# Seven half-size products with three accumulating on one bank and fewer sums on DVE

## Chip, cores and metric

The kernel runs on one core of a Trainium2 chip. The metric is the device time of one execution in microseconds; the medians below are over three runs.

## What is computed

Causal attention with a decay (2 x 8 heads, 576 positions, width 64), then a mixture of 4 experts (1152 tokens, 512 wide, 1024 inner), then a gated layer (inner width 1536). Cut to the layers that the change touches:

```python
def _moe_ref(x, domain_probs, w1, w2):
    p = domain_probs / (domain_probs.sum(-1, keepdims=True) + 1e-09)
    out = np.zeros((N, D), dtype=np.float32)
    for e in range(E):
        h = np.maximum(x @ w1[e], 0.0)
        out += p[:, e:e + 1] * (h @ w2[e])
    return out
def _moe2_ref(x, w_gate, w_val, w_out):
    g = x @ w_gate
    silu = g * (1.0 / (1.0 + np.exp(-g)))
    return (silu * (x @ w_val) @ w_out).astype(np.float32)
```

## The kernel before

Every float32 operand is split into a high and a low part, and each product is three matmuls (high x high, high x low, low x high). The inner width is worked in pieces of 256, the tokens in two halves of 512 and 640. A *stage* is one piece of width and one half of the tokens: the inward products x @ w (its items), then the outward products (6 matmuls for each 128 tokens, in two items of 3). The first stages belong to the mixture, the last ones to the gated layer; below these are called the first and the second stage of the kernel.

An inward product [256 wide x 512 deep] x [512 deep x tokens] is done as a 2 x 2 block product in seven half-size products instead of eight (`seven`, L1070): the weights' and x's halves and their sums are made ahead, and the seven results are added up to the four blocks c11, c12, c21, c22 of the result, which lie side by side in one SBUF tile "cc". The intermediate sums are called u1, u2, u3, u4. Each of the seven products is 6 matmuls of 256 or 320 columns (half of the tokens' half) into a PSUM bank of its own ("h", five banks in rotation). Product 0 is copied out to u1 by ACT or DVE; the other results are added on DVE straight from their banks: c11 = u1 + 1, u2 = u1 + 2, u4 = u2 + 3, u3 = u2 + 4, c12 = u4 + 5, c22 = u4 + 4, c21 = u3 + 6 (`total`, L1108, and the lambda at L1132): seven DVE sums and a copy for each set. `rest` then works on each half of "cc": relu and split in the first stage (`moe1_seven`, L1204), sigmoid, multiply and split in the second (`moe2_in`, L1341), where a stage has two sets, gate and value.

The order of the work is written out while the kernel is built: a greedy planner (`Plan`) holds a clock for each engine with cost estimates, takes the task that can start first (rank settles ties), and lets a copy marked "av" go to the engine that bids less, ACT or DVE (`held`, 1 us in this part, is added to DVE's bid). After an operation a dependent one on another engine, or on the same engine other than PE, is taken to be ready LINK later (0.13 us for ACT and DVE, 0.2 for PE). A `Ring` is the planner's count of free buffers: `take` needs a free one, `give` hands one back. PE's own order is fixed: each item hangs on the last (`dense_pe`, L960).

In `stages` (L1427) the inward items of a stage are merged with the outward items of the stage before: `merge` (L99) spreads the inward items evenly from 0 to 1 and the outward ones from 0.75 to 1 (LAG). So in a first-stage set five products come first, then an outward item, product number five, more outward items, product six, and the rest. In a second-stage stage the seven gate products come without outward items between them, and the value products from the fourth on with them. Stages of a piece that was begun before all tokens were there have fewer outward items to merge. The first piece of the second stage and the last stage have orders of their own (L1453 to L1464).

Of the kernel before, what the change touches and what calls it, by code (L numbers as in the profile page):

```python
# [8 lines left out]
F32 = mybir.dt.float32  # L9
# [8 lines left out]
P = 128  # L18
# [3 lines left out]
HALF = 512  # L22
# [258 lines left out]
def attention_moe_swiglu(ctx, tc, q_early, q_late, k, v, s, dp, w1, w2, wg, wv, wo, out):  # L281
# [691 lines left out]
    def needs_x(t0, t1):  # L973
        if t0 in x_ready:
            return x_ready[t0]
        return [x for g in range(len(groups)) if place[g] < t1 for x in done_x[g]]
# [88 lines left out]
        late["sums"] = [x for y in done.values() for x in y]  # L1065


    SEVEN = [((0, 0), (0, 0)), ((0, 1), (1, 0)), (0, 1), (2, 0), (1, 2), (3, (1, 1)), ((1, 1), 3)]

    def seven(w, st, rest):  # L1070


        t0, n = st.t0, (st.t1 - st.t0) // 2
        box, done, banks = {}, {}, {}
        x_ = late["T", t0]

        def item(i):
            A, X = SEVEN[i]

            def run():  # L1080
                hp = banks[i] = bank("h")[:, :n]
                for c in range(2):
                    if isinstance(A, tuple):
                        wh, wl = (y[:, 2 * A[1] + c, A[0] * P:A[0] * P + P] for y in w.ops)
                    else:
                        wh, wl = (y[:, A, c, :] for y in w.sums)
                    if isinstance(X, tuple):
                        a = t0 + X[1] * n
                        h, l = (y[:, 2 * X[0] + c, a:a + n] for y in (xh, xl))
                    else:  # L1090
                        h, l = (x_[y][:, X, c, :] for y in "hl")
                    nc.tensor.matmul(hp, wh, h, start=c == 0, stop=False)  # L1092
                    nc.tensor.matmul(hp, wh, l, start=False, stop=False)  # L1093
                    nc.tensor.matmul(hp, wl, h, start=False, stop=c == 1)  # L1094

            def make(last):
                deps = [w.done[A[1]] if isinstance(A, tuple) else w.sums_done[A]]
                deps += needs_x(t0, t0 + 2 * n) if isinstance(X, tuple) else x_["done"][X]
                give = [(w.first, w.parts_ring), (w.first, ring("ws"))] if last and i == 6 else []
                done[i] = t = dense_pe(6 * pe(n), run, deps, take=[ring("h")], give=give)  # L1100
                finish(i, t)
                return t
            return make

        def part(k):
            return box["c"][:, k * n:k * n + n]

        def total(k, x, i, deps, spent=False):  # L1108

            def run():  # L1110
                nc.vector.tensor_tensor(part(k), part(x), banks[i], op=ALU.add)  # L1111
            return add("dve", 0.12 + 0.00113 * n, run, deps, give=[(done[i], ring("h"))] if spent else [], rank=prompt())


        def finish(i, t):
            if i == 0:
                def copy(on):
                    box["c"] = late["t"].tile([P, 2 * (N - HALF)], F32, name="cc", tag="cc", bufs=2)[:, :4 * n]
                    move(on, part(1), banks[0])
                done["u1"] = any_of("av", "bank", n, copy, [t], take=[ring("cc")], give=[(t, ring("h"))], rank=prompt())  # L1120
            elif i == 1:
                done["c11"] = total(0, 1, 1, [t, done["u1"]], True)
            elif i == 2:
                done["u2"] = total(1, 1, 2, [t, done["c11"]], True)
            elif i == 3:
                done["u4"] = total(3, 1, 3, [t, done["u2"]], True)
            elif i == 4:
                done["u3"] = total(2, 1, 4, [t, done["u2"]])
            elif i == 5:
                done["c12"] = total(1, 3, 5, [t, done["u4"], done["u3"]], True)  # L1130
                rest(0, [done["c11"], done["c12"]], done["u1"], lambda: box["c"], n)
                done["c22"] = add("dve", 0.12 + 0.00113 * n, lambda: nc.vector.tensor_tensor(part(3), part(3), banks[4], op=ALU.add),  # L1132
                                  [done["c12"]], give=[(done[4], ring("h"))], rank=prompt())
            elif i == 6:
                c21 = total(2, 2, 6, [t, done["u3"]], True)
                rest(1, [done["c22"], c21], done["u1"], lambda: box["c"], n)
        return [item(i) for i in range(7)]

    def order(st):

# [200 lines left out]
    def moe2_in(wgt, wvt, st):  # L1341
# [22 lines left out]
        def val(f, deps, owner, src, n):  # L1364
# [11 lines left out]
            lows.append(st.lows[f, st.t0, 2 * n])  # L1376
            if len(lows) == 2:
                add(None, 0.0, None, lows, give=[(box["ts"], ring("sg")), (owner, ring("cc"))])
        return seven(wgt, st, gate) + seven(wvt, st, val)

    def moe2_out(w, st, first, last):
        items = []
# [44 lines left out]
    def stages():  # L1427
# [3 lines left out]
        for i, t0, t1, lastone in jobs():  # L1431
# [21 lines left out]
            if i == 1000 and t0 == 0:  # L1453

                items = items[:3] + prev + items[3:]
            elif i == 1000:

                items = [items[x] for x in (0, 1, 7, 8)] + merge(items[2:7] + items[9:], prev)
            elif i == 1000 + len(wide) - 1 and t0:
                items = items + prev  # L1460
            elif prev:
                items = merge(items, prev)
# [125 lines left out]
```

## Time and profile before

| | us |
|---|---|
| runs | 717.32, 718.48, 718.18; median 718.18 |
| the profiled execution | 719.07 |
| its span from the first to the last instruction | 717.2 |
| PE busy | 698.9 (97%) |
| DVE busy | 557.2 (78%) |
| ACT busy | 358.2 (50%) |
| POOL busy | 463.2 (65%) |

Attention takes the span's first part; the first set of seven products starts at 198.7 us, the second stage at about 492 us. In the rows, "h" is a bank for inward products and "o" one for outward products; "cc" is the tile of the four blocks; "hh" and "hl" are mostly the high and low part of the inner activations; "wah", "wsh" and the like are parts of weights and of their sums; "acc_a" and "acc_b" are the output's accumulators. L1092 to L1094 are the matmuls of a set, L1154 to L1156 those of an outward item, L1111 and L1132 the DVE sums, L327 a copy on ACT. A matmul's busy time runs to its modelled end, and the next one starts before that, so the pace of PE is read from starts.

### The profile page before, as it was taken

The numbers are of one execution on the slowest core, as the hardware profiler recorded it, in microseconds if no ns is written. First come the engines' busy times: TensorE is split into PE (matmuls) and PEld (weight loads), VectorE is DVE, ScalarE is ACT, GpSimd is POOL, SyncE is SP. The second block draws the span as 40 slices with busy tenths as digits, with TensorE's granted clock in tenths as the row PEclk, the third lists the DMA queues.
The fourth block names the chain that finished last, engine by engine and source line by source line (L and its number), as shares of the span: only waits on it lengthen the run. The fifth ranks groups of instructions, "written<-read, shape, count | busy, mean of one in ns | idle before, by whom it ended". The sixth has DMA issues, their size and how long they took to land.

```text
span 717.2 us, 11928 instructions
## 1 busy us (share of the span) xinstructions
PE 698.9 (97%) x4280; PEld 607.2 (85%) x4280; DVE 557.2 (78%) x1081; ACT 358.2 (50%) x757; POOL 463.2 (65%) x436
## 2 busy tenths in 40 slices
PE   8899999999999999999999999999999999999997
PEld 6676666787898989898989888997989999999996
DVE  5686575797278899999999999766884777787665
ACT  5787777423444545555565654655644424233210
POOL 3743242599366667666767678799899868585321
PEclk9999999999999999999999999999999999999999
DMA  8794642112204445465446553222121202010003
GB/s 206 241 306 125 205 135 85 31 58 71 106 0 148 147 157 168 147 207 166 147 160 194 188 186 103 65 86 89 39 80 31 82 23 74 30 31 1 1 1 133
DMA packets 31452, 79.80 MB, mean 111 GB/s; under 512 B 3568, under 2 KB 9216, under 8 KB 31392
## 3 DMA queue, kind: packets, MB, share of 16 engines
q1 hardware_dynamic: 31248, 78.90, 34.4%
q8 instruction: 34, 0.56, 0.3%
q14 instruction: 26, 0.21, 0.1%
q10 hardware_dynamic: 144, 0.13, 0.1%
HBM read 67.16 MB, written 11.85 MB: 110 GB/s over the span
## 4 chain that ended last, share of the span: by engine, by line
PE 74%; DVE 12%; POOL 5%; issue 4%; ACT 4%; DMA 0%; DVEq 0%; ACTq 0%; POOLq 0%
PE h L1092 10%; PE h L1094 10%; PE h L1093 10%; PE o L1154 10%; PE o L1155 10%; PE o L1156 10%; PE tp L598 2%; PE po L657 2%; PE sp L527 2%; DVE tt L1031 1%; ACT ns L553 1%; PE h L992 1%; DVE cc L1111 1%; PE h L994 1%; PE h L993 1%
## 5 line engine op out<-in xcount | busy, mean ns | idle before, releaser
L1111 DVE TENSOR_TENSOR cc<-cc,h 128x320 f32<-128x320 f32 (+1 forms) x282 | 124.9, 452 | 49.3 <-PE h L1094 43.0
L1154 PE MATMUL o<-woh,hh 128*128 128x512 f32 x396 | 157.3, 397 | 2.9 <-DVE acc_a L1242 1.6
L1156 PE MATMUL o<-woh,hl 128*128 128x512 f32 x396 | 154.7, 391 | 1.7 <-DVE hl L340 1.7
L1155 PE MATMUL o<-wol,hh 128*128 128x512 f32 x396 | 155.8, 393 | 0.0
L1092 PE MATMUL h<-xh,wsh 128*128 128x320 f32 (+1 forms) x312 | 92.9, 298 | 0.0
L1094 PE MATMUL h<-xh,wsl 128*128 128x320 f32 (+1 forms) x312 | 92.8, 297 | 0.0
L1093 PE MATMUL h<-xl,wsh 128*128 128x320 f32 (+1 forms) x312 | 92.7, 297 | 0.0
L340 POOL TENSOR_TENSOR wal<-raw,wah 128x512 fp32r<-128x512 f32 (+1 forms) x58 | 70.8, 1230 | 32.4 <-ACT wah L327 31.4
L1156 PEld LDWEIGHTS o<-woh,hl 128*128 128x128 f32 x396 | 74.4, 188 | 18.6 <-DVE hl L340 2.1
L340 POOL TENSOR_TENSOR wol<-raw,woh 128x512 fp32r<-128x512 f32 x54 | 79.2, 1475 | 15.0 <-ACT woh L327 14.5
L1154 PEld LDWEIGHTS o<-woh,hh 128*128 128x128 f32 x396 | 74.5, 188 | 16.6 <-DVE acc_a L1242 2.3
L1155 PEld LDWEIGHTS o<-wol,hh 128*128 128x128 f32 x396 | 74.5, 188 | 10.8
L1211 ACT ACTIVATE cc<-cc 128x640 f32<-128x640 f32 (+1 forms) x46 | 32.1, 698 | 91.7 <-DVE cc L1111 91.6
L340 POOL TENSOR_TENSOR hl<-cc,hh 128x512 fp32r<-128x512 f32 (+1 forms) x28 | 41.9, 1498 | 52.8 <-ACT hh L1214 52.6
L1092 PE MATMUL h<-xh,wah 128*128 128x320 f32 (+1 forms) x234 | 69.4, 297 | 0.0
L1094 PE MATMUL h<-xh,wal 128*128 128x320 f32 (+1 forms) x234 | 69.4, 296 | 0.0
L1093 PE MATMUL h<-xl,wah 128*128 128x320 f32 (+1 forms) x234 | 69.3, 296 | 0.0
L340 POOL TENSOR_TENSOR wsl<-sf,wsh 128x512 fp32r<-128x512 f32 x44 | 66.8, 1537 | 0.8 <-ACT wsh L327 0.8
L1242 DVE SCALAR_TENSOR_TENSOR acc_b<-o,pr,acc_b 128x512 f32<-128x512 f32 x75 | 55.5, 743 | 8.4 <-PE o L1156 8.1
L1092 PEld LDWEIGHTS h<-xh,wsh 128*128 128x128 f32 x312 | 58.9, 189 | 1.5
L1093 PEld LDWEIGHTS h<-xl,wsh 128*128 128x128 f32 x312 | 59.0, 189 | 1.4
L1094 PEld LDWEIGHTS h<-xh,wsl 128*128 128x128 f32 x312 | 59.0, 189 | 0.0
(146 smaller groups left out, 1667.8 us busy)
## 6 DMA issues: line engine op xcount, KB each, us to landing
raw<-in_w SPq DMA_DIRECT2D x42, 512.0 KB, 5.0
n<-hl SPq DMA_DIRECT2D x36, 256.0 KB, 2.3
raw<-n SPq DMA_DIRECT2D x18, 512.0 KB, 3.3
hh<-in_wg SPq DMA_DIRECT2D x12, 512.0 KB, 4.2
hh<-in_wv SPq DMA_DIRECT2D x12, 512.0 KB, 4.0
hh<-in_wo SPq DMA_DIRECT2D x12, 512.0 KB, 3.9
dql<-rows SPq DMA_DIRECT2D x8, 512.0 KB, 5.1
vr<-in_v SPq DMA_DIRECT2D x4, 640.0 KB, 4.4
```

What stands on the lines that cost most here:

```text
L340: {"v": nc.vector, "p": nc.gpsimd}[e].tensor_tensor(to, x, f32(y), op=ALU.subtract)
L527: nc.tensor.matmul(sp[j][:, at:at + w], Q[half[j], x], K[half[j], :w], start=True, stop=False)
L598: nc.tensor.transpose(tp[:kn, x * P:x * P + P], box["ns"][lane][:, at + c * P:at + c * P + kn], ident)
L1092: nc.tensor.matmul(hp, wh, h, start=c == 0, stop=False)
L1093: nc.tensor.matmul(hp, wh, l, start=False, stop=False)
L1094: nc.tensor.matmul(hp, wl, h, start=False, stop=c == 1)
L1111: nc.vector.tensor_tensor(part(k), part(x), banks[i], op=ALU.add)
L1154: nc.tensor.matmul(op, hh[:, f, ts], wh[:, f, :], start=f == 0, stop=False)
L1155: nc.tensor.matmul(op, hh[:, f, ts], wl[:, f, :], start=False, stop=False)
L1156: nc.tensor.matmul(op, hl[:, f, ts], wh[:, f, :], start=False, stop=f == NF - 1)
L1211: nc.scalar.activation(src()[:, o], src()[:, o], AF.Relu)
L1242: nc.vector.scalar_tensor_tensor(acc(t), bank_(), sc, acc(t), op0=ALU.mult, op1=ALU.add)
```

## The change

Products 0, 2 and 3 go onto one bank. Product 0 is copied out as u1; product 2 then accumulates onto the same bank, which so holds u2, and is copied out; product 3 accumulates onto that, which gives u4, and is copied out. The DVE sums u2 and u4 are no more, and two copies come, free for ACT or DVE. In the first stage (`join`) product 6 accumulates onto the bank of product 4 once c22 has read it, which makes the sum u3 unnecessary: four DVE sums. In the second stage u3 stays as a sum and product 6 has its own bank: five DVE sums. Each accumulating product waits for the read before it (`READ`). The order of the seven is 0, 1, 5, 2, 4, 3, 6 instead of 0 to 6. The first piece of the second stage gets another order for its second half. Cut to its core:

```diff
+    TURN = (0, 1, 5, 2, 4, 3, 6)
     SEVEN = [((0, 0), (0, 0)), ((0, 1), (1, 0)), (0, 1), (2, 0), (1, 2), (3, (1, 1)), ((1, 1), 3)]
 
-    def seven(w, st, rest):
+    def seven(w, st, rest, join=True):
...
+        ONTO = (None, None, 0, 0, None, None, 4 if join else None)
+        READ = ((), (), ("u1",), ("u2",), (), (), ("c22",) if join else ())
...
             def run():
-                hp = banks[i] = bank("h")[:, :n]
+                if ONTO[i] is None:
+                    banks[i] = bank("h")[:, :n]
+                hp = banks[i] = banks[i if ONTO[i] is None else ONTO[i]]
...
-                    nc.tensor.matmul(hp, wh, h, start=c == 0, stop=False)
-                    nc.tensor.matmul(hp, wh, l, start=False, stop=False)
-                    nc.tensor.matmul(hp, wl, h, start=False, stop=c == 1)
+                    for x, (a, b) in enumerate(((wh, h), (wh, l), (wl, h))):
+                        nc.tensor.matmul(hp, a, b, start=not x and not c and ONTO[i] is None, stop=x == 2 and c == 1, skip_group_check=i in (0, 2, 3) or join and i in (4, 6))
...
+                deps += [done[x] for x in READ[i]]
...
-                done[i] = t = dense_pe(6 * pe(n), run, deps, take=[ring("h")], give=give)
+                done[i] = t = dense_pe(6 * pe(n), run, deps, take=[ring("h")] if ONTO[i] is None else [], give=give)
...
+        def taken(k, i, deps, **kw):
+
+            def copy(on):
+                if "c" not in box:
+                    box["c"] = late["t"].tile([P, 2 * (N - HALF)], F32, name="cc", tag="cc", bufs=2)[:, :4 * n]
+                move(on, part(k), banks[i])
+            return any_of("av", "bank", n, copy, deps, rank=prompt(), **kw)
 
         def finish(i, t):
             if i == 0:
...
+                done["u1"] = taken(1, 0, [t], take=[ring("cc")])
             elif i == 1:
-                done["c11"] = total(0, 1, 1, [t, done["u1"]], True)
+                done["c11"] = total(0, 1, 1, [t, done["u1"]], 1)
             elif i == 2:
-                done["u2"] = total(1, 1, 2, [t, done["c11"]], True)
+                done["u2"] = taken(2, 2, [t])
             elif i == 3:
-                done["u4"] = total(3, 1, 3, [t, done["u2"]], True)
-            elif i == 4:
-                done["u3"] = total(2, 1, 4, [t, done["u2"]])
-            elif i == 5:
-                done["c12"] = total(1, 3, 5, [t, done["u4"], done["u3"]], True)
+                done["u4"] = taken(3, 3, [t], give=[(done[0], ring("h"))])
+                done["c12"] = total(1, 3, 5, [done["u4"], done["c11"], done[5]], 5)
                 rest(0, [done["c11"], done["c12"]], done["u1"], lambda: box["c"], n)
...
+                done["c22"] = total(3, 3, 4, [done["c12"], done[4]])
+                if not join:
+                    done["u3"] = total(2, 2, 4, [done["c22"]], 4)
             elif i == 6:
-                c21 = total(2, 2, 6, [t, done["u3"]], True)
-                rest(1, [done["c22"], c21], done["u1"], lambda: box["c"], n)
-        return [item(i) for i in range(7)]
+                done["c21"] = total(2, 2, 6, [t, done["c22" if join else "u3"]], 4 if join else 6)
+                rest(1, [done["c22"], done["c21"]], done["u1"], lambda: box["c"], n)
+        return [item(i) for i in TURN]
...
-        return seven(wgt, st, gate) + seven(wvt, st, val)
+        return seven(wgt, st, gate, False) + seven(wvt, st, val, False)
...
-                items = [items[x] for x in (0, 1, 7, 8)] + merge(items[2:7] + items[9:], prev)
+                items = items[:3] + merge(items[3:], prev)
```

## Rows read from the trace of the kernel before

**Rows 1.** The page's part 1: busy us, share of the span, instructions.
```profile
PE 698.9 (97%) x4280; PEld 607.2 (85%) x4280; DVE 557.2 (78%) x1081; ACT 358.2 (50%) x757; POOL 463.2 (65%) x436
```

**Rows 2.** PE's waits from 198 us on: line, releaser, us, times, longest.
```profile
PE o L1156 <- DVE hl L340: 1.7, 1, 1.7
PE o L1270 <- DVE xl L1281: 1.5, 1, 1.5
PE h L1092 <- DVE cc L1111: 1.0, 1, 1.0
PE o L1154 <- DVE acc_b L1242: 0.4, 1, 0.4
PE o L1154 <- DVE acc_a L1242: 0.3, 1, 0.3
PE h L1092 <- ACT cc L327: 0.2, 1, 0.2
```

**Rows 3.** Table of stretches: us, busy by engine (x), PEclk, DMA share, GB/s.
```profile
198.00:500.00 302.00, 299.33 (x1738) 268.74 (x1736) 268.76 (x417) 163.19 (x297) 218.93 (x182) 1.00 0.43 140
500.00:545.00 45.00, 42.41 (x285) 39.61 (x286) 35.62 (x67) 23.68 (x52) 43.04 (x44) 1.00 0.20 60
545.00:717.00 172.00, 168.53 (x1055) 156.26 (x1053) 120.40 (x210) 50.02 (x96) 100.60 (x87) 1.00 0.12 39
```

**Rows 4.** Groups by line and shape: count, busy us, mean ns, idle before.
```profile
L1111 DVE TENSOR_TENSOR cc<-cc,h 128x320 f32<-128x320 f32 x156 | 74.2, 483 | 31.3 <-PE h L1094 26.8 <-ACT cc L327 0.8 <-ACT woh L327 0.7
L1111 DVE TENSOR_TENSOR cc<-cc,h 128x256 f32<-128x256 f32 x126 | 50.7, 414 | 18.1 <-PE h L1094 16.2
```

**Rows 5.** Timeline, gate set at 320 columns: start, us, engine, line, tiles.
```profile
588.09 0.31 PE L1094 MATMUL h<-xh,wsl 128*128 128x320 f32 x1
588.44 0.49 DVE L1111 TENSOR_TENSOR cc<-cc,h 128x320 f32<-128x320 f32 x1 [0.39 <-PE h L1094]
588.97 0.31 PE L1094 MATMUL h<-xh,wsl 128*128 128x320 f32 x1
```

**Rows 6.** Timeline, gate set at 256 columns.
```profile
568.82 0.37 ACT L327 COPY cc<-h 128x256 f32<-128x256 f32 x1 [0.26 <-PE h L1094]
...
570.58 0.28 PE L1094 MATMUL h<-xh,wsl 128*128 128x256 f32 x1
...
571.30 0.28 PE L1094 MATMUL h<-xh,wsl 128*128 128x256 f32 x1
```

**Rows 7.** Timeline around a PE wait for a copy, ACT, PEld and PE.
```profile
519.37 0.42 ACT L327 COPY cc<-h 128x320 f32<-128x320 f32 x1
519.84 0.19 PEld L1092 LDWEIGHTS h<-xh,hl 128*128 128x128 f32 x1 [0.49 <-ACT cc L327]
519.84 0.42 PE L1092 MATMUL h<-xh,hl 128*128 128x320 f32 x1 [0.23 <-ACT cc L327]
```

**Rows 8.** Timeline, late set of the first stage, PE and DVE.
```profile
449.40 0.31 PE L1094 MATMUL h<-xh,wsl 128*128 128x320 f32 x1
450.70 0.40 PE L1156 MATMUL o<-woh,hl 128*128 128x512 f32 x1
450.94 0.30 PE L1092 MATMUL h<-xh,wah 128*128 128x320 f32 x1
...
450.27 0.49 DVE L1132 TENSOR_TENSOR cc<-cc,h 128x320 f32<-128x320 f32 x1
450.68 0.74 DVE L1242 SCALAR_TENSOR_TENSOR acc_a<-o,pr,acc_a 128x512 f32<-128x512 f32 x1
```

**Rows 9.** Timeline near the end, POOL and PE.
```profile
705.70 1.56 POOL L340 TENSOR_TENSOR hl<-sg,hh 128x640 fp32r<-128x640 f32 x1 [1.53 <-ACT hh L327]
707.70 0.39 PE L1156 MATMUL o<-woh,hl 128*128 128x512 f32 x1
```

**Rows 10.** Timeline, turn between the stages, PE and ACT.
```profile
532.45 0.28 PE L1094 MATMUL h<-xh,wal 128*128 128x256 f32 x1
...
534.11 0.39 ACT L327 COPY cc<-h 128x256 f32<-128x256 f32 x1
```

More of the change, by code (lines that the diff above doesn't have):

```diff
@@ L1106, in part, with total @@
             return box["c"][:, k * n:k * n + n]
-        def total(k, x, i, deps, spent=False):
+        def total(k, x, i, deps, spent=None):
             def run():
                 nc.vector.tensor_tensor(part(k), part(x), banks[i], op=ALU.add)
-            return add("dve", 0.12 + 0.00113 * n, run, deps, give=[(done[i], ring("h"))] if spent else [], rank=prompt())
+            return add("dve", 0.12 + 0.00113 * n, run, deps, give=[] if spent is None else [(done[spent], ring("h"))], rank=prompt())
@@ L1115, in finish @@
+        def taken(k, i, deps, **kw):
[4 more added lines that the diff above has]
+            return any_of("av", "bank", n, copy, deps, rank=prompt(), **kw)
         def finish(i, t):
             if i == 0:
-                def copy(on):
-                    box["c"] = late["t"].tile([P, 2 * (N - HALF)], F32, name="cc", tag="cc", bufs=2)[:, :4 * n]
-                    move(on, part(1), banks[0])
@@ L1120, in finish @@
-                done["u1"] = any_of("av", "bank", n, copy, [t], take=[ring("cc")], give=[(t, ring("h"))], rank=prompt())
+                done["u1"] = taken(1, 0, [t], take=[ring("cc")])
             elif i == 1:
-                done["c11"] = total(0, 1, 1, [t, done["u1"]], True)
+                done["c11"] = total(0, 1, 1, [t, done["u1"]], 1)
             elif i == 2:
-                done["u2"] = total(1, 1, 2, [t, done["c11"]], True)
+                done["u2"] = taken(2, 2, [t])
             elif i == 3:
-                done["u4"] = total(3, 1, 3, [t, done["u2"]], True)
-            elif i == 4:
-                done["u3"] = total(2, 1, 4, [t, done["u2"]])
-            elif i == 5:
-                done["c12"] = total(1, 3, 5, [t, done["u4"], done["u3"]], True)
+                done["u4"] = taken(3, 3, [t], give=[(done[0], ring("h"))])
@@ L1131, in finish @@
+                done["c12"] = total(1, 3, 5, [done["u4"], done["c11"], done[5]], 5)
                 rest(0, [done["c11"], done["c12"]], done["u1"], lambda: box["c"], n)
-                done["c22"] = add("dve", 0.12 + 0.00113 * n, lambda: nc.vector.tensor_tensor(part(3), part(3), banks[4], op=ALU.add),
-                                  [done["c12"]], give=[(done[4], ring("h"))], rank=prompt())
+                done["c22"] = total(3, 3, 4, [done["c12"], done[4]])
+                if not join:
+                    done["u3"] = total(2, 2, 4, [done["c22"]], 4)
```

## The prediction

> **What bounds the kernel now.** I read the busy line of the page first: PE is busy 97% of the span, DVE 78%, ACT 50% [rows 1]. Then the table of stretches, cut where the sets of seven products run: from 198 us on PE is busy 510.3 of 519 us at full granted clock, while DVE is at 89% (268.8 of 302) in the first stage, 79% in the turn from one stage to the other and 70% (120.4 of 172) in the last; ACT is at 54%, 53% and 29% [rows 3]. So PE is the bound, and its instruction count doesn't change: 47 sets of 42 matmuls stay. The only room is PE's waits, so the list of these came third: six single waits after 198 us, 1.7 + 1.5 + 1.0 + 0.4 + 0.3 + 0.2 = 5.1 us, five of them on DVE, one on ACT [rows 2]. A wait also lays the weight load open: the matmul after the wait at 519.84 takes 0.42 us, where one in a stream takes 0.31 [rows 5, 7]; with the matmul that follows about 0.2 us for each, 1.2 in all. So 6.3 us is the most that the change can win, 0.9%, unless it makes PE's stream itself shorter, which it doesn't.
>
> **What leaves and what comes.** The first stage has 23 sets, the second 24 (6 pieces of width, 2 halves of the tokens, gate and value). Of 7 DVE sums 4 are left in the first and 5 in the second: 3 x 23 + 2 x 24 = 117 sums go, 66 at 320 columns (0.483 us) and 51 at 256 (0.414) [rows 4]: 31.9 + 21.1 = 53 us off DVE, an eighth of its 425 us in this part. Two copies a set come, which the planner gives to ACT unless ACT is far behind (HELD2 adds 1 us to DVE's bid): 52 x 0.42 + 42 x 0.37 = 37 us on ACT [rows 6, 7], which has the room on average. All of this lies beside PE; what matters is which waits go and which come.
>
> **Waits that can go (gains).** Evictions of bank "o" that DVE does late, 0.4 + 0.3, with their weight loads 1.1 us: they come from DVE's backlog in the first stage, and a sum fewer in three should end most; I take 0.8 (0 to 1.1). The wait of 1.7 for "hl" has a chain through DVE, ACT and DVE again, behind integer work of the narrowing that stays; I take 0.8 (0 to 1.9). The 1.5 for "xl" hangs on the transposes of the turn, which no sum feeds; 0.3 (0 to 1.7). The two waits for a bank "h", 1.0 + 0.2, with their loads 1.6: a set takes 4 or 5 banks instead of 7, so these as such go: 1.6. Sum 3.5 us.
>
> **Waits that come (losses).** Each accumulating product now waits for a copy, and PE is in order: all that is behind it waits too, both products and output matmuls.
>
> *Product 3 behind the copy of u2.* Product 4 lies between. At 320 columns a product's last matmul starts at 588.09 and ends at 588.40; a reader reacts in 0.04 (the sum at 588.44) [rows 5]; the copy takes 0.42, and PE's weight load starts 0.05 after its end (519.79 to 519.84) [rows 7]: 588.91. The weight load of the product after the next goes with the matmul at 588.97 [rows 5]. So 0.06 us are left. At 256 columns: 570.58 + 0.28 + 0.04 + 0.37 + 0.05 = 571.32, wanted at 571.30 [rows 6]: 0.02 late, or some 0.05 with a slower reaction. This holds where nothing else is merged in between: the 12 gate sets, and two value sets (the first piece's first half and the last of all). In the first stage and in the other value sets at least one output item of 3 x 0.24 us (450.70 to 450.94 for one of its matmuls [rows 8]) lies between as well, so some 0.7 us is left. The same gap again: five banks are taken by a set of the second stage, so the value's product 0 takes the bank of the gate's product 0, free only after the copy of u4, with product 6 between: 12 more. 26 places in all, half at 256 columns: 13 x 0.05 = 0.7 us if ACT is idle; when ACT is in the middle of another operation, up to that one's length each (0.4 us and more). ACT at 29% there [rows 3] speaks for the low end: 0.7 (0 to 4).
>
> *Product 6 behind c22 (first stage only).* The chain is product 3, copy of u4, c12, c22. In 21 of the 23 sets five or more output items (15 x 0.24 = 3.6 us) lie between 3 and 6, enough: 0.04 + 0.42 + 0.05 + 0.48 + 0.74 + 0.48 + 0.05 = 2.3 us, with an eviction of 0.74 between the sums [rows 4, 7, 8]. An integer operation of the narrowing in front as well takes it to the edge in some: 0.4 us in all (0 to 3). In two sets, of stages that have only four output items to merge, two lie between. There (rows of 449.4 on, where the last matmul of the product in this place ends at 449.71): copy until 450.17, c12 until 450.71, eviction until 451.45, c22 until 451.9; product 6 wants its weight load at 450.70 [rows 8]. Wait 1.2 us; 0.4 if c22 goes ahead of the eviction. The planner takes the eviction first, as it adds 0.13 us (LINK) behind c12 and the eviction is ready by then. 2 x 1.2 = 2.4; but the first of the two stands just ahead of the "hl" wait of 1.7, in which part of it drowns: 1.8 (0.6 to 2.6).
>
> *Product 2 behind the copy of u1.* Two products lie between, so one more (0.72 or 0.88 us [rows 5, 6]) than above: 0.7 to 0.9 us beyond the copy. In the turn between the stages ACT is often later: at 534.11 the copy starts 1.38 us after product 0 ends (532.73) [rows 10]. With three such places, and u2 and u4 in the same queue behind casts: 1.5 us (0 to 3).
>
> *The end.* In the last stage value product 3 ends where 5 did, but c12 waits for a copy (0.5 us more) and u3 is one more sum (0.45) ahead of c21, whose multiply, cast and low part end in "hl" at 707.26; the matmul that reads it starts at 707.70, its load a matmul (0.24) earlier [rows 9]. 0.9 late against 0.2 of room: 0.7 at most, nothing if the planner gives the multiply to POOL, idle there: 0.4.
>
> *Orders that move.* Product 5 is third now and needs weight sum 3 two places earlier; weights are made up to four ahead (AHEAD) and before their stage begins, so nothing. In the second stage's first piece product 5 leads instead of 2 (own quarter of x instead of a sum: earlier ready), and in its second half three products lead instead of four; sums of x are ready before. Nothing, from -0.5 to 0.5. No DMA and no SP instruction moves.
>
> Losses: 0.7 + 0.4 + 1.8 + 1.5 + 0.4 = 4.8 us. Net 4.8 - 3.5 = +1.3. The profiled execution is 719.07 (span 717.2 and 1.9 around it), so 720.4 for it; the median is 0.9 lower, and the forecast for it 718.18 + 1.3 = 719.5.
>
> The Trainium skill, Perfetto Trace Analysis, Optimizing Tensor Performance, speaks against this change: independent matmul groups should rotate through different banks so that the reading of one overlaps the next. The rows agree so far that a product in a stream has 0.06 us left at best; what the rule would make of the time is rival (e). The same page, Optimizing Scalar/DVE Operations, says that work of a full DVE may well go to ScalarE, which is the case for it; DVE here is full only in part of the first stage.
>
> **Rivals.** (a) *Relief wins.* DVE's backlog sets all five DVE waits, the copies find ACT idle, and c22 goes ahead: gains 5.5 (all but part of "xl"), losses 0.4 + 0 + 0.8 + 0.7 + 0.4 = 2.3: -3.2, 715.0. For it: 89% on DVE in the first stage. Against: six waits in 519 us show that the planner already keeps the backlog off PE. (b) *The joined bank is the new bound.* In the dense part of the first stage, where DVE is fullest, c22 comes behind narrowing and evictions in most of the 21 sets; from a lag of about 3.4 us on it holds PE, and at 0.2 us in each this adds 4: 723.5. (c) *Nothing to speak of*: copies hidden, waits where they were: 718.2 +- 1. (d) *The clock falls.* With short waits in each set the granted clock could go to its lower level, 1.2 of 2.4 GHz; against it, it was 1.00 in all three stretches, the one with the waits of 1.7 and 1.5 us too [rows 3]. The 42.4 us of PE work in the middle stretch at half speed would be +42: 760. The Trainium skill, TensorE: Matmul & The Clock Gate, A second HAM failure mode, tells of a kernel whose cycling through banks made the clock swing; the trace here shows none of it. (e) *Bare copies.* Were nothing of a copy hidden, each of some 117 new waits (2 a set, 23 more at product 6) would cost 0.42 + 0.09: 60 us, 778. Against it, a product of 0.72 or 0.88 us lies between in all of them [rows 5, 6].
>
> **How the numbers follow.** Forecast (waits trade places, 718.0 to 721.5): 0.44, half of it under 719.6. (a) 0.30, (b) 0.16, (c) 0.09, (d) and (e) together 0.01. A measurement here tells 0.2% (1.4 us) from no change. Faster by more: (a) and a little of (c), 0.31. Within: half the forecast and most of (c), 0.30. Slower: the other half, (b), (d) and (e), 0.39. Range from (a) to (b): 714.8 to 723.5; the forecast alone 718.0 to 721.5.
>
> **What would show it.** DVE near 504 us and ACT near 395 on the page; 212 DVE sums and 141 copies; no wait of PE for "h" on DVE's sums but at product 6; two waits of about 1.2 us at product 6 in the stages around 430 and 450 us; waits of under 0.1 us on ACT's copies in the gate sets after 545 us. I am wrong if PE's waits after 198 us add up to under 3 us (a), or if product 6 waits in most sets of the first stage (b), or if the granted clock is under 1.

## The result, and the profile after

The changed kernel takes 725.45 us (median of four runs, 724.97 to 726.25) against 718.33 for the kernel before beside it: 1.0102 times as long, interval 1.0084 to 1.0119. The same kernel again, in a later comparison with more runs: 723.79 against 717.99, 1.0082 (1.0065 to 1.0099). So it is slower by some 6 to 7 us, where 719.5 was forecast, with 723.5 as the upper end.

The page of the changed kernel, part 1 (busy us, share of the span, instructions), answers to [rows 1]:

```profile
PE 706.4 (98%) x4280; PEld 609.2 (84%) x4280; DVE 531.4 (73%) x978; ACT 393.2 (54%) x851; POOL 449.6 (62%) x422
```

Groups by line and shape, after (L1116 the DVE sums, L327 the copies out of the banks of a set; x is their count, then busy us and mean ns), against [rows 4]:

```profile
L1116 DVE TENSOR_TENSOR cc<-cc,h 128x320 f32<-128x320 f32 x116 | 54.5, 481 | 48.7 <-ACT cc L327 42.9 <-PE h L1098 4.1 <-ACT woh L327 0.3
L1116 DVE TENSOR_TENSOR cc<-cc,h 128x256 f32<-128x256 f32 x96 | 38.7, 413 | 18.2 <-ACT cc L327 11.9 <-PE h L1098 5.1
L327 ACT COPY cc<-h 128x320 f32<-128x320 f32 x78 | 33.1, 425 | 71.2 <-PE h L1098 71.0
L327 ACT COPY cc<-h 128x256 f32<-128x256 f32 x63 | 23.3, 370 | 44.3 <-PE h L1098 43.4 <-DVE acc_a L1396 0.6
```

212 sums and 141 copies, at the prices of before, and ACT at 393: the change does what it says. But DVE fell by 26 us, not by the 53 of its sums: POOL fell by 14 as well, so the planner laid part of its work into the room on DVE.

The table of stretches after (us, busy by engine with counts, granted clock, DMA share, GB/s), against [rows 3], and the list of PE's waits from 198 us on (line, releaser, us, times, longest), against [rows 2]:

```profile
198.00:500.00 302.00, 297.62 (x1721) 264.72 (x1720) 251.92 (x357) 177.69 (x342) 200.89 (x170) 1.00 0.42 140
500.00:545.00 45.00, 43.59 (x285) 39.48 (x285) 34.70 (x59) 28.58 (x64) 41.98 (x42) 1.00 0.19 60
545.00:724.00 179.00, 175.07 (x1082) 160.87 (x1081) 113.87 (x177) 67.21 (x136) 107.50 (x88) 1.00 0.11 38
```

```profile
PE h L1098 <- DVE cc L1116: 3.4, 9, 0.7
PE h L1098 <- ACT cc L327: 1.3, 3, 0.6
PE o L1161 <- DVE acc_a L1249: 0.7, 1, 0.7
PE o L1163 <- POOL hl L340: 0.6, 1, 0.6
PE o L1277 <- DVE acc_a L1249: 0.3, 1, 0.3
```

From 198 us on the granted clock is 1.00 in each stretch. Of the waits of [rows 2] the two long ones (1.7 for "hl", 1.5 for "xl") are gone. In their place stand nine short ones of product 6 for c22, three for copies, two for late evictions, one at the end. The sum of the waits rose only from 5.1 to 6.3 us, but their number from 6 to 15. By the starts each delays PE by some 0.27 us more than its row says: at 281.47 the row has 0.34, and 0.61 is lost. A matmul's modelled end lies 0.16 us behind the start of the next (0.28 against a pace of 0.12 at 256 columns), and the open weight load adds 0.1. Nine more waits make 2.4 us of that, where the prediction's 0.2 for each would make 1.8. Waits add up by number as well as by length, and a lateness of under 0.16 us stands in no row of the list: the second stage's 1.5 us below is of that kind.

**Where the time went.** The starts of each set's first matmul, read from the two timelines set by set, give the shift of after against before. Ahead of the first set, where both programs are the same, the profiled execution is 1.7 us late. That is the scatter of the run's start: in the second profile of the same kernel the first set starts 2.9 us earlier, and the shifts that follow are the same within about 0.1. Part of it may be the granted clock: in the first profile it is 0.64 from 9 to 12 us and 0.50 from 27 to 30, in the second 1.00 in both. From the first set on, in us (the first stage up to the set at 492 us, the turn up to 550, the second stage up to 695, then the end, which is PE's last matmul):

| kernel | first stage | turn | second stage | end | sum by the traces | measured, median against before |
|---|---|---|---|---|---|---|
| after | +3.6 | -0.6 | +1.5 | +0.9 | +5.4 | +7.1 |
| after_again | +3.7 | -0.6 | +1.5 | +0.9 | +5.5 | +5.8 |

In the first stage the shift rises by 0.5 to 0.74 us in each of seven 256-column sets, the first at 222 us in the kernel before and the last at 388 (an eighth, at 246, gains 0.5), and stays where it is in the 320-column sets between them. The timeline of one of these sets, after (start, us, engine, line; PE's other rows are left out): the last matmul of its product 3, the copy of u4, what DVE does, and product 6:

```profile
276.63 0.28 PE L1098 MATMUL h<-xh,wsl 128*128 128x256 f32 x1
276.95 0.37 ACT L327 COPY cc<-h 128x256 f32<-128x256 f32 x1 [1.19 <-PE h L1098]
277.28 1.01 DVE L764 CUSTOM_DVE_ANT_0 hl<-hl 128x1024 uint16<-128x1024 uint16 x1
278.33 1.11 DVE L767 SCALAR_TENSOR_TENSOR hl<-hh,hl 128x512 int32<-128x512 int32 x1
279.36 0.74 DVE L1249 SCALAR_TENSOR_TENSOR acc_b<-o,pr,acc_b 128x512 f32<-128x512 f32 x1
280.02 0.40 DVE L1116 TENSOR_TENSOR cc<-cc,h 128x256 f32<-128x256 f32 x1
280.35 0.74 DVE L1249 SCALAR_TENSOR_TENSOR acc_b<-o,pr,acc_b 128x512 f32<-128x512 f32 x1
281.01 0.40 DVE L1116 TENSOR_TENSOR cc<-cc,h 128x256 f32<-128x256 f32 x1
281.47 0.38 PE L1098 MATMUL h<-xh,wah 128*128 128x256 f32 x1 [0.34 <-DVE cc L1116]
281.69 0.28 PE L1098 MATMUL h<-xl,wah 128*128 128x256 f32 x1
```

The copy is in time (it begins 0.04 after the last matmul of product 3 ends). But while it runs, DVE takes up two operations of the narrowing (2.1 us) and an eviction, in the order that the planner wrote for it, so c12, which could begin at 277.3, begins at 280.02. Another eviction goes between c12 and c22, and product 6 waits 0.34, its weight load open behind that. The chain from product 3 to product 6 takes 4.6 us here; 2.3 was reckoned with, and without a wait product 6 starts 3.9 us after product 3 (the set at 198 us).

### The profile page after: what moved, and what is told of

It is laid out like the page before. It is cut to its first block, busy times and chain, and to the rows that moved or that the text cites. A ratio compares the mean times of both kernels' runs of the same rounds, so it can differ in the third digit from the quotient of the medians.

```text
span 724.3 us, 11845 instructions
## 1 busy us (share of the span) xinstructions
PE 706.4 (98%) x4280; PEld 609.2 (84%) x4280; DVE 531.4 (73%) x978; ACT 393.2 (54%) x851; POOL 449.6 (62%) x422
## 4 chain that ended last, share of the span: by engine, by line
PE 67%; DVE 14%; POOL 6%; ACT 5%; DMA 4%; issue 3%; POOLq 0%; SPq 0%; DVEq 0%; ACTq 0%
PE h L1098 29%; PE o L1161 9%; PE o L1162 9%; PE o L1163 9%; PE po L657 2%; PE tp L598 2%; DMA dqe<-rows 2%; PE sp L527 2%; DVE tt L1031 2%; PE h L992 1%; DVE acc_b L1249 1%; DVE hl L758 1%; DVE hl L340 1%; DVE hl L764 1%; PE h L993 1%
## 5 line engine op out<-in xcount | busy, mean ns | idle before, releaser
L1116 DVE TENSOR_TENSOR cc<-cc,h 128x320 f32<-128x320 f32 (+1 forms) x212 | 93.1, 450 | 66.9 <-ACT cc L327 54.9
L327 ACT COPY cc<-h 128x320 f32<-128x320 f32 (+1 forms) x141 | 56.4, 400 | 115.5 <-PE h L1098 114.4
L340 POOL TENSOR_TENSOR hl<-cc,hh 128x512 fp32r<-128x512 f32 (+1 forms) x19 | 27.1, 1427 | 52.5 <-ACT hh L1221 52.5
```

Of the source, the lines that this page charges most:

```text
L327: nc.scalar.copy(to, x)
L340: {"v": nc.vector, "p": nc.gpsimd}[e].tensor_tensor(to, x, f32(y), op=ALU.subtract)
```

## The experiments

All kernels compute the whole of the reference. The "turn_" kernels take the changed order of products (0, 1, 5, 2, 4, 3, 6), the "join" kernels the joined bank of 4 and 6, "pair" means that c12 and c22 are one task on DVE with nothing between them. The shifts are worked out from the timelines as above. With each edit the planner writes the order of all engines anew, so a kernel differs from its neighbour in more than the edit, and the sums by the traces and the times differ by up to 1.4 us.

| kernel | first stage | turn | second stage | end | sum by the traces | measured, median against before | ratio, interval |
|---|---|---|---|---|---|---|---|
| nojoin | +2.7 | +0.8 | +1.5 | +0.9 | +5.8 | +6.3 | 1.0077 to 1.0115 |
| first_only | +3.6 | -1.8 | 0 | 0 | +1.8 | +2.3 | 1.0022 to 1.0052 |
| second_only | -0.4 | -0.4 | +1.4 | +0.9 | +1.5 | +0.7 | 1.0006 to 1.0030 |
| join_only | -1.6 | -0.9 | 0 | 0 | -2.5 | -2.8 | 0.9949 to 0.9977 |
| turn_join | +3.6 | -0.3 | 0 | 0 | +3.3 | +4.1 | 1.0035 to 1.0067 |
| pair | -0.8 | -1.7 | +1.4 | +0.9 | -0.2 | +0.9 | 0.9998 to 1.0018 |
| tail_old | +3.7 | -0.5 | +1.4 | 0 | +4.6 | +4.9 | 1.0052 to 1.0081 |
| pair_first | -1.1 | +0.5 | 0 | 0 | -0.6 | -0.9 | 0.9977 to 0.9996 |
| turn_pair | +4.3 | -0.8 | 0 | 0 | +3.5 | +2.2 | 1.0024 to 1.0048 |
| second_turn | +0.7 | +2.8 | +2.0 | 0 | +5.5 | +4.4 | 1.0056 to 1.0081 |
| nojoin_pair | +1.7 | -0.5 | +1.5 | +0.9 | +3.7 | +3.9 | 1.0044 to 1.0068 |
| turn_first | +3.3 | -1.3 | 0 | 0 | +2.0 | +2.6 | 1.0027 to 1.0055 |
| m6_late | +13.6 | -1.4 | +1.5 | +0.9 | +14.6 | +16.0 | 1.0208 to 1.0238 |
| join_pair | -2.1 | -1.9 | 0 | 0 | -4.0 | -2.7 | 0.9946 to 0.9971 |

### Which part, which stage

**nojoin**: product 6 on a bank of its own in the first stage.

```diff
-        return seven(w, st, rest)
+        return seven(w, st, rest, False)
```

> The change, but with product 6 of the first stage's 23 sets on a bank of its own again (product 4's bank is read by c22 and u3 and given back; five sums a set, as in the second stage). Theory T1, the joined bank (product 6 stands behind the chain copy of u4, c12, c22, with narrowing work and evictions let in between) costs 3.9 to 4.5 us in the first stage: then the time is 721 to 722, the wait of PE for 'h' on DVE's sums falls from 3.4 us to under 1, and the first products of the 256-column sets between 233 and 430 us keep the shift that the kernel before has, within 0.5 us. Rival R1, the two copies a set (one bank for products 0, 2 and 3) cost the time wherever they are: 724.5 to 726, the 3.4 us turn into waits on ACT's copies. Rival R2, it was the start of the run (the 1.7 us by which the changed kernel was late already at 200 us): 725 as well, with the 1.7 us there again.

724.83 us: theory T1 fell. The waits for c22 are gone, but the time isn't. R2 falls too, as the first set starts 0.9 us earlier here than in the kernel before. The longest of PE's waits from 198 us on in this kernel:

```profile
PE h L1098 <- ACT cc L327: 1.6, 3, 0.7
PE o L1163 <- DVE hl L340: 1.5, 2, 1.0
PE o L1161 <- DVE acc_b L1249: 1.2, 2, 0.7
PE h L1098 <- DVE cc L1116: 1.2, 1, 1.2
```

What comes late now is what PE waits for: the low part "hl", evictions, and in the turn a sum (1.2 us). That they are late because c22 and c21 are is likely, and tested by nojoin_pair below. R1 had the time right but named the copies, which make 1.6 us of these waits.

**first_only** and **second_only**: one stage new, the other as before (the order of the first piece of the second stage goes with the second).

> New sets (joined bank and copies) in the first stage only; the second stage's 24 sets and their order are those of before. T1 with the rest of the theory (second stage and end cost 2.0 to 2.5 us by tight copies): 722.5 to 724, with waits at product 6 as in the changed kernel and none on copies after 545 us. Rival R1' (the second stage costs nothing, all of the 7 us comes from the first stage and the turn): 725 to 726.

> The first stage's 23 sets as before (seven sums, seven banks), the second stage's 24 sets new (copies, one bank for 0, 2 and 3). The theory (first stage 4 to 5 us, second stage and end 2.0 to 2.5): 720 to 721, with PE's waits for 'h' on ACT's copies and the one near the end back again. Rival: no cost in the second stage, 718 to 718.7; rival: the second stage costs more than the shift of its sets shows, since the first stage's relief hid part: over 722.

720.84 and 719.29. The first is 1.7 us under its range, as the old turn keeps the 1.3 us of the "xl" wait that the new one wins and loses again: in the changed kernel the shift falls from 3.6 to 2.3 where that wait stood and is back at 3.7 a set later, behind a copy (0.58 us of wait at 516.93) and shorter delays. The second is under its 720 too: up to 550 us it is 0.9 ahead of the kernel before. The two together give 3.0 of the 7.1 (5.8 on the second reading), 3.3 by the traces; most of the rest is the turn, in which both new parts meet.

**after_again**, the changed kernel unchanged:

> The changed kernel as it is, once more. In its trace the sets of products account for 5.4 us (from the first set's start at about 200 us to the end, against the same stretch of the kernel before); another 1.7 us lay ahead of the first set, where both programs are the same. If these 1.7 us are the scatter of the run's start: 723.5 to 724.7 here. If they belong to the change: 725 to 726.

723.79: the start's 1.7 us were scatter.

### The joined bank and the order

**join_only**: the kernel before, with product 6 on the bank of product 4 and u3 gone, in the first stage; order and sums as before.

```diff
-                hp = banks[i] = bank("h")[:, :n]
+                hp = banks[i] = banks[4] if i == 6 else bank("h")[:, :n]
...
+                deps += [done["c22"]] if i == 6 else []
...
-            elif i == 4:
-                done["u3"] = total(2, 1, 4, [t, done["u2"]])
```

> The kernel before in all but one thing: in the first stage product 6 accumulates on product 4's bank after c22 has read it, and the sum u3 goes (six sums a set; one copy as before, products 0 to 5 on banks of their own, old order of products). If the join alone is what costs (product 6 directly behind a chain of two sums, c12 and c22): 721.5 to 724, with waits of PE for 'h' on c22. If it needs the copy of u4 in the chain as well (the hop through ACT lets narrowing and evictions in ahead of c12): 718 to 719.5. In the old order product 5, the last before 6, is itself read by c12, so a set whose output items lie elsewhere would wait 1 us and more; the range goes up to 726.

715.74, faster than before by 0.37% and under every number expected: the join alone is a gain. The timeline of the same set in this kernel, product 5 (last before 6 here), c12, c22 and product 6:

```profile
274.56 0.28 PE L1163 MATMUL h<-xh,wsl 128*128 128x256 f32 x1
275.33 0.41 DVE L1181 TENSOR_TENSOR cc<-cc,h 128x256 f32<-128x256 f32 x1
277.13 0.40 DVE L1200 TENSOR_TENSOR cc<-cc,h 128x256 f32<-128x256 f32 x1
278.82 0.28 PE L1161 MATMUL h<-xh,wah 128*128 128x256 f32 x1
```

c12 begins 0.5 us after product 5, as u4 has long been there, c22 ends at 277.53, and product 6 comes 1.3 us later. A narrowing operation and an eviction go in between c12 and c22 here too; there is room for them. In the changed kernel the product in this place is 3, and u4 must still be taken from it before c12 can begin.

**turn_join**: the same with the changed order of products, u2 and u4 still sums, a bank each.

```diff
-        return [item(i) for i in range(7)]
+        return [item(i) for i in (0, 1, 5, 2, 4, 3, 6)]
```

> The kernel with the joined bank alone (product 6 on product 4's bank, u3 gone, u2 and u4 as DVE sums, a bank each for 0, 2 and 3), but in the first stage with the products in the changed kernel's order (0, 1, 5, 2, 4, 3, 6). Theory T2, the copies on one shared bank cost the 5 us by which the changed first stage is behind the joined bank alone: 715 to 717. Rival T3, the order costs it (with product 3 last but one, c12 and c22 both start only after it, one step of the chain later than with product 5 in its place): 718.5 to 721, with waits for 'h' on c22 in most of the 256-column sets.

722.09, 1.1 us over T3's numbers: the order turns a gain of 2.8 us into a loss of 4.1, with no shared bank for 0, 2 and 3 and no added copy. 3.1 us of waits on c22 in eight places are there again, five of them in the nine 256-column sets. With copies and shared bank in the same order (first_only) the first stage loses the same 3.6 us, so these two have no net cost there.

**turn_first**: the kernel before with only the order changed, in the first stage; no join.

> The kernel before with nothing changed but the order of products in the first stage (0, 1, 5, 2, 4, 3, 6; seven sums, a bank for each, no joined bank, one copy). If the order by itself makes c12 and c22 late and that costs, joined or not: 721 to 724. If the order costs only by product 6 waiting for c22 on the joined bank: 717.5 to 719.5.

720.61, +2.6: 0.4 us under the first theory's numbers and 1.1 over the second's. So the order costs without the join as well, but less, and in other places. Up to the set at 400 us the shift is 1.2 us here and 3.8 in turn_join. Another 2.8 come in one place, at the wait for the low part at 437.76 and in the fall of the clock behind it (some 1.5 us, last section). The two longest rows of PE's waits:

```profile
PE o L1224 <- DVE hl L340: 2.2, 1, 2.2
PE o L1222 <- DVE acc_b L1310: 1.9, 3, 0.9
```

Four kernels that differ from before in these two things alone, and only in the first stage, in us against before: old order, separate banks 0; old order, joined -2.8; new order, separate +2.6; new order, joined +4.1. The join gains where c22 is early and costs where it is late.

### What stands between the links

**pair**: the changed kernel with c12 and c22 as one task in the joined sets.

```diff
-                done["c12"] = total(1, 3, 5, [done["u4"], done["c11"], done[5]], 5)
+                def two():
+                    nc.vector.tensor_tensor(part(1), part(3), banks[5], op=ALU.add)
+                    nc.vector.tensor_tensor(part(3), part(3), banks[4], op=ALU.add)
+                done["c12"] = done["c22"] = add("dve", 0.24 + 0.00226 * n, two, [done["u4"], done["c11"], done[5], done[4]], give=[(done[5], ring("h"))], rank=prompt())
```

> The changed kernel, with c12 and c22 as one task on DVE in the joined sets, so that no eviction and no narrowing comes between the two. The seven waits of 0.35 us in the 256-column sets, where an eviction stands between (280.35 to 281.09 in the trace after), should go, as c22 ends 0.74 earlier: 4 us less if all of the 0.6 a set goes, so about 3.5 us below the changed kernel of the same call. If the lateness is already there when c12 begins (the copy, then two narrowing operations ahead of it), 0 to 1 us.

718.90, 4.9 us under the changed kernel of the same comparison. The timeline of the same set:

```profile
276.65 1.11 DVE L767 SCALAR_TENSOR_TENSOR hl<-hh,hl 128x512 int32<-128x512 int32 x1
277.68 0.74 DVE L1255 SCALAR_TENSOR_TENSOR acc_b<-o,pr,acc_b 128x512 f32<-128x512 f32 x1
278.35 0.41 DVE L1138 TENSOR_TENSOR cc<-cc,h 128x256 f32<-128x256 f32 x1
278.78 0.42 DVE L1139 TENSOR_TENSOR cc<-cc,h 128x256 f32<-128x256 f32 x1
279.28 0.36 PE L1098 MATMUL h<-xh,wah 128*128 128x256 f32 x1
```

The narrowing and the first eviction still go ahead of c12, but c22 follows it at once, and product 6 shows no wait. Its first matmul takes 0.36 us where one in a stream takes 0.28, and such a set still loses 0.2 us, where it lost 0.66. Waits on c22 fall from 3.4 us in nine places to 0.5 in two. By the shifts 2.4 us of the gain stand in the 256-column sets up to 400 us, where the eviction of 0.74 us went from between two sums; the rest came later, in sets and a turn that the planner ordered anew.

**m6_late**: the changed kernel with product 6 two output items (1.4 us) later on PE, in the first stage's sets.

```diff
+            if i < 1000 and "h" in late and prev:
+                at = [y for y, x in enumerate(items) if x[0] in tails][0]
+                items.insert(min(at + 2, len(items) - 1), items.pop(at))
```

> The changed kernel with product 6 of the first stage's sets two output items (1.4 us of PE work) later. If only product 6's place is at fault: the nine waits on c22 go, 719 to 720.5, about 4 under the changed kernel. If c22's lateness costs whoever comes after it (c21 and the relu, cast and low part behind it are later still by 1.4): 722 to 725, with waits on 'hl', 'hh' or evictions in their place.

734.02, well beyond both theories' numbers, on the side of the second. The longest of PE's waits:

```profile
PE o L1163 <- DVE hl L340: 4.4, 4, 1.3
PE o L1163 <- POOL hl L340: 3.1, 3, 2.2
PE o L1161 <- ACT hh L1221: 1.9, 2, 1.1
PE h L1098 <- ACT cc L327: 1.7, 3, 0.9
PE o L1161 <- DVE acc_b L1249: 1.5, 1, 1.5
```

The waits on c22 are all but gone (one of 0.03 us at 442.27), and the low part of what product 6 produced is late instead. Some 1.5 us more are a fall of the clock (last section). Product 6 is held from both sides: c22 ahead of it and c21, relu, cast and low part behind it, which the next outward products want. Neither a bank of its own (nojoin) nor a later place helped; a shorter chain did (pair).

**nojoin_pair**, **turn_pair**, **join_pair**: the pair in nojoin, in turn_join and in join_only.

> The changed kernel with a bank of its own for product 6 in the first stage (the version that was no faster than the changed kernel), with c12 and c22 as one task. If lateness of c22 itself costs (what follows it: relu, cast, low part, evictions), not only the wait of product 6: 720 to 722, 3 to 5 under that version. If the pair works only by product 6's wait: as that version, 724 to 725.5.

> As the kernel with the joined bank alone in the changed order (u2 and u4 as DVE sums, a bank each for 0, 2 and 3), with c12 and c22 as one task. Theory T3, the order makes c12 and c22 late and what DVE puts between them decides: 715 to 717, as without the order, 4 to 6 us under the same kernel with two tasks. If the order costs in another way (banks that 5 and 4 hold longer, DVE fuller than with copies): 719 to 722. Against the first stage with copies and the pair it tells what the copies on one bank are worth by themselves: T2 (copies cost) 1 us and more for this one, T3 no more than 1 either way.

> The joined bank alone with the old order of products and c12 and c22 as one task. With the old order two of the waits were for c22 and the turn (0.6, 1.3): 715 to 716, as without the pair, if the pair only mends what the order spoils; under 714 if it is a gain of its own.

nojoin_pair: 722.32, 2.4 under nojoin by the differences to before: in the direction of the first theory (an early c22 is worth something without a joined bank too), short of its 3 to 5. turn_pair: 720.57, 1.9 under turn_join by the differences to before, where 4 to 6 were expected, so T3's number is missed. But up to the set at 400 us, through all of the 256-column sets of the first stage, the pair gives the same in three kernels: the shift goes from 3.9 to 1.5 us with copies (after, pair), from 3.8 to 1.4 with sums (turn_join, turn_pair) and from 3.4 to 1.0 without the join (nojoin, nojoin_pair). There an early c22 is worth 2.4 us whatever else the set does. The kernels part only behind 400 us: from there to 492 us pair gains another 2.4 against before, while turn_pair loses 2.8, with 1.1 us of wait on one eviction and 1.4 on c22 in two late sets. Why the later sets answer so differently stays open. join_pair: 715.30, as join_only (715.74, in another comparison) within the intervals; its trace is 1.5 us ahead of join_only's, which the times don't confirm. So with the old order the pair gains little or nothing. It mends what the order spoils.

**pair_first**: the pair in the first stage, the second stage as before.

> The first stage of the changed kernel with c12 and c22 as one task, the second stage and its order as before. The pair brought the first stage from 2.3 us behind the kernel before (at the set that starts at 508 us) to 2.1 ahead; the old second stage adds none of the 2.2 us that the new one lost. Theory: 715.3 to 716.5, about 2.3 under the kernel before. Rival: the turn needs the new second stage's relief of DVE, then 717 to 719.

717.47, the rival's number: the turn took back most of what the first stage had won (a shift of -2.4 us at 508 us, -0.6 at 550). One wait of 2.06 us for a copy stands at 518.44, and the clock falls behind it (see the last section).

### The second stage and the end

**second_turn**: the first stage as before, the second in the changed order with sums and a bank for each.

> The first stage as before; in the second stage the changed order of products (0, 1, 5, 2, 4, 3, 6), but with sums and a bank for each, no copies but u1. If the 1.3 us of the second stage's 256-column sets come from copies that are some 0.05 us late on the shared bank: those sets here run as before, 0 +- 0.1 each. If they come from the order: 0.2 to 0.4 in each pair of 256-column sets again. The end: 0.9 if product 3 in product 5's place makes c12 late, 0 if the copy does. In all 717.5 to 719.5.

722.76, by the differences to before 3.6 us over second_only, and far over the 719.5 expected. Without the shared bank a product of the second stage waits for a free bank, which the late c12 and c22 hold longer:

```profile
PE h L1161 <- DVE cc L1180: 3.3, 6, 1.3
```

So the shared bank and its copies are the better way to have this order there. With them the cost is starts that are late by too little for the list of waits. After 550 us they stand in three places of the 256-column sets, after. In the gate set product 3 starts late behind the copy of u2 (576.20), as the prediction described. In the value set product 5 starts late (579.18): by the rotation of the five banks it takes the one that the gate's c12 reads, and c12 comes late on DVE, from 578.72 to 579.12. Then the copy of u1 begins behind the sigmoid's activation, and the weights of product 2 are loaded 0.05 us after its end:

```profile
576.20 0.39 PE L1098 MATMUL h<-xh,wsh 128*128 128x256 f32 x1
579.15 0.63 ACT L1358 ACTIVATE sg<-cc 128x512 f32<-128x512 f32 x1 [1.57 <-DVE cc L1116]
579.18 0.39 PE L1098 MATMUL h<-xh,wsh 128*128 128x256 f32 x1
579.69 0.36 ACT L327 COPY cc<-h 128x256 f32<-128x256 f32 x1
580.10 0.19 PEld L1098 LDWEIGHTS h<-xh,wsh 128*128 128x128 f32 x1 [0.16 <-ACT cc L327]
```

By the starts the three places cost some 0.15, 0.12 and 0.22 us, so about 0.5 us in the two 256-column sets of a piece together, in three pieces; the 320-column sets lose nothing in the traces.

**tail_old**: the changed kernel with the last two sets as before.

> The changed kernel, with the very last two sets (gate and value of the last stage) as they were before. If the copy and the additional u3 in the last value set cost the 0.9 us seen at the end (wait of 0.58 on the low part at 714.69): 0.9 us under the changed kernel of the same call. If something else is late there, the same time.

722.88, 0.9 under the changed kernel of the same comparison: the end's 0.9 us is the copy and the added u3 in the last value set. In the changed kernel POOL's low part starts at 713.08 and PE waits for it:

```profile
713.08 1.55 POOL L340 TENSOR_TENSOR hl<-sg,hh 128x640 fp32r<-128x640 f32 x1 [2.13 <-ACT hh L327]
714.69 0.50 PE L1163 MATMUL o<-woh,hl 128*128 128x512 f32 x1 [0.58 <-POOL hl L340]
```

## Why the prediction was wrong, point by point

- **What bounds it** held: PE's instructions are the same 4280, and the whole difference lies in its waits, the open weight loads behind them and starts that are a little late. The limit of 6.3 us for a gain wasn't reached by any kernel; join_pair, the best, shows 4.0 by its trace and 2.7 by the times.
- **What leaves and comes** held in counts, prices and ACT's total. "DVE near 504" did not: 531, as the planner moved work to DVE.
- **Product 6 behind c22, 0.4 in 21 sets (0 to 3)** is the term that failed, and its mechanism was there: rival (b), given 0.16. It was priced on a chain of 2.3 us with one eviction between the sums. In the trace two narrowing operations and another eviction go in as well, 4.6 us. The prediction had called one such operation "the edge in some" sets; it is the rule in the 256-column ones. Seven of them wait about 0.35 us each, and one 320-column set 0.33 (468.77); by the starts each loses some 0.6, 5.1 us in all instead of 0.4. The shift is 3.9 us at the set at 400 us, as the set at 246 gains 0.5. Rival (b) had 4 from 0.2 in each set.
- **"Orders that move. Nothing"** is the step at the root of it. The prediction followed product 5, which moved to an earlier place, and found it ready. That product 3 takes its place as the last one before 6, and that its result must pass u4 first, it priced for product 6's wait alone, not for c12, c22 and what hangs on them. The new order alone, in the first stage, costs 2.6 us (turn_first; some 1.5 of it the fall of the clock in the profiled execution), and with it the join's gain of 2.8 turns into a loss of 4.1 (turn_join).
- **The two sets with little to merge, 1.8 (0.6 to 2.6)**: one of the two waits came, at 436.54 (0.71, 1.0 by the starts). In the other set product 6 stands behind four transposes, which wait for an accumulator (0.32 at 455.69), and it doesn't wait for c22. So 1.0 instead of 2.4.
- **26 tight places, 0.7 (0 to 4)**: at 320 columns the room of 0.06 us was enough, as worked out. After 550 us three of the places at 256 columns show, product 3 of the gate sets: some 0.45 us together. The rest of the second stage's 1.5 stands where the prediction had room or saw nothing: product 2 behind the copy of u1 (0.65, put at 0.7 to 0.9 to spare) and the value's product 5 behind the bank of the gate's late c12 (0.35). That 1.5 lies in the term's range is luck.
- **The turn, 1.5 (0 to 3)**: -0.6 with the gains on "xl" (1.3) and on the two waits for a bank (2.0 by the starts) in it, so the losses there are some 2.7, near the top of the range. **The end, 0.4 (0.7 at most)**: 0.9, over its bound.
- **Gains, 3.5**: "hl" gave its whole 1.7 and "xl" 1.3, more than the 0.8 and 0.3 taken; the second came back as a loss in the set behind it. The evictions' 0.8 did not come: 0.7 and 0.3 of waits for them stand in after too. The waits for a bank "h" went as expected.
- **The Trainium skill**, Perfetto Trace Analysis, Optimizing Tensor Performance, was put as speaking against the change (groups should rotate through banks). No net cost of the shared bank shows: in the first stage the loss is 3.6 us with it (first_only) and with a bank for each (turn_join), and in the second stage 1.4 with it (second_only) and 2.0 without (second_turn).
- **Rival (d)**, the clock: not in the changed kernel, whose rows show 1.00 in all three stretches from 198 us on.

By the traces the terms add to 5.4; of the 7.1 measured first, the rest is scatter, as the second reading of 5.8 shows. The forecast's 1.3 misses that by about 4; product 6 alone is 4.7 over its term.

The version that beats both kernels is the join without the order: join_only, 715.74 (0.9949 to 0.9977), or join_pair, 715.30 (0.9946 to 0.9971).

What stays open: why the pair's gain of 2.4 us up to 400 us is lost behind it where u2 and u4 are sums and doubled where they are copies, and which of the copies makes the turn lose in the changed kernel what the old second stage keeps there.

## What to carry to other kernels

When products change places, ask what the last one before a wait must still pass through, not only whether the one moved is ready: a link more at the end of a chain let the ready operations of a busy engine in ahead of what follows (here 2.1 us of narrowing and two evictions). Price such a chain with all that the engine has ready, and where it decides, tie the links into one task. Before joining two results on one bank, look at both sides of the joined product: with the old order it had 1.3 us of room, with the new one none on either side.

## What the runs showed that was not expected

The granted clock, 1.00 in the changed kernel from 198 us on, fell in three experiments behind a wait. In pair_first PE waited 2.06 us at 518.44; the table of stretches shows the clock fall and return:

```profile
515.00:518.00 3.00, 1.37 (x10) 1.11 (x8) 2.02 (x4) 1.18 (x3) 3.00 (x3) 1.00 0.00 0
518.00:521.00 3.00, 2.56 (x14) 2.56 (x15) 1.93 (x5) 1.24 (x4) 3.00 (x3) 0.80 0.49 180
521.00:524.00 3.00, 3.00 (x15) 3.00 (x15) 2.96 (x5) 1.42 (x3) 3.00 (x4) 0.63 0.00 0
524.00:528.00 4.00, 4.00 (x23) 3.54 (x22) 1.15 (x3) 1.10 (x2) 3.78 (x5) 1.00 0.02 5
```

in m6_late behind a wait of 2.17 us for "hl" at 424.92:

```profile
426.00:429.00 3.00, 3.00 (x13) 2.55 (x12) 0.63 (x2) 0.38 (x1) 2.84 (x4) 0.56 0.86 251
```

and in turn_first behind a wait of 2.24 us for "hl" at 437.76, the row of the timeline and then the stretches behind it:

```profile
437.76 0.50 PE L1224 MATMUL o<-woh,hl 128*128 128x512 f32 x1 [2.24 <-DVE hl L340]
```

```profile
439.00:442.00 3.00, 3.00 (x9) 2.32 (x8) 3.00 (x4) 1.25 (x2) 2.00 (x3) 0.52 0.14 52
442.00:446.00 4.00, 4.00 (x21) 3.46 (x20) 2.70 (x5) 0.65 (x2) 0.00 (x0) 1.00 0.60 197
```

0.52 is close to the lower of the two levels, 1.2 of 2.4 GHz. In the kernel before the wait of 1.7 us at the same place left the clock at 1.00, from 436 to 439 us and from 439 to 443. The fall is short: eight matmuls of 512 columns start some 0.42 us apart instead of 0.23 (the last at 441.98), so it cost an estimated 1.5 us, on top of the wait.

The second thing is how alike executions are once the first set has begun: two profiles of the changed kernel differ by 2.9 us at that point and their shifts by about 0.1 from there on, so set-by-set shifts tell a few tenths of a microsecond apart where medians of whole runs don't.
